# Pairing heads a and a+4: two tokens to a packet, w_in in halves of its rows, batches in half as many transfers

## The chip, the cores and the metric

The kernel runs on one core of a Trainium2 chip. A core has five engines with instruction queues of their own: TensorE (PE, matmuls), VectorE (DVE), ScalarE (ACT), GpSimd (POOL) and SyncE (SP), which here only sends transfers to the 16 DMA engines. The metric is the device time of one execution in microseconds; lower is better.

## The reference

Attention in chunks of 64 tokens, then an FFN with a SoLU and a layer norm, all in float32 (w_in and w_out are handed over as float64):

```
q, k, v: (8 batches, 8 heads, 576 tokens, 64)     chunk = 64 tokens
scores = q_c @ k_c^T / 8;  attn = softmax(scores);  out = attn @ v_c
x = out, heads side by side: (4608 tokens, 512)
h = x @ w_in                      # 512 x 1024
solu = h * softmax(h)
ln = (solu - mean) / sqrt(var + 1e-6) * g_ln
y = ln @ w_out                    # 1024 x 512
```

## The kernel before

The 4,608 tokens are 36 tiles of 128 tokens, two chunks each; nine chunks are a batch, so tile 4 (and every ninth after it) straddles two batches. All eight heads of a tile are worked on together.

Each tile goes through these steps. q and k are brought into a layout with the head dimension on the partitions (`QT`, `KT`: 128 partitions are two heads of 64, four such pairs side by side). `scores` makes 32 matmuls of 64x64x64, a softmax follows, the attention is turned, and `values` makes 32 more matmuls with v. The result is x of the tile, 512 values on four groups of 128 partitions; a group is one pair of heads, and w_in's rows are cut into four units of 128 rows to match. `ffn_in` multiplies x by w_in in 24 matmuls of 512 columns: both operands are split into a high and a low part, and three products are summed (tiles 0 and 1 take one product in plain float32 instead). SoLU, norm and turning of z follow on the other engines, and `ffn_out` makes 24 matmuls with w_out, in three thirds.

q and k reach `QT` and `KT` in one of two ways. Tiles 0 to 9 are loaded in their natural layout (`load_natural`, into the two slots of `nat`): a partition is a token, and each token and head is one run of 256 bytes. TensorE turns them (`turn_natural`, four transposes of 128x128 for q and four for k), and ScalarE or VectorE copies the result out of PSUM. From tile 10 on, whole batches are staged (`qk_loads` into `q_st` and `k_st`, two buffers each): 32 transfers a batch, one for each tensor, head and half of the head dimension, each to 32 partitions and in runs of 128 bytes; VectorE turns 32x32 blocks of them (`qk_turn`).

w_in and w_out are 4 MB each as float64. `load_pair(x)` loads a unit of 1 MB into a raw tile (x = 0 to 3 is w_in, 4 to 7 w_out; unit 0 in two transfers of half the columns). `unit_scale`, `unit_round`, `unit_high` and `unit_rest` turn a unit into its float32 value and its parts, on GpSimd, VectorE and ScalarE.

What runs when is written out by hand. Every engine works through its instructions in program order. Up to the fifth tile the order is the string `START`: each word is a step and its arguments, looked up in `todo`, and a word that comes again resumes that step behind its next `yield`. `n:i` loads natural tile i, `N:i:x` turns its q or k, `P:x` loads a unit, `v:i` loads v, `S` scores, `A`, `B` softmax, `T` turns the attention, `V` values, `M` FFN-in (M:0 in four parts, one for each unit, so it needs all four units by its end), `X`, `Y`, `z` SoLU and z, `F` a third of FFN-out, `Q:b` lists a batch's transfers and `q:n` sends n of them, `W` are matmuls with no use but to keep TensorE busy. All loads but a few go through SyncE, in the order of these words. `early` holds the two transfers of unit 0, which the words `P0` and `P1` send.

From tile 5 on a loop does the rest. An iteration sends v of a later tile, `LOADS[0]` transfers of the batch list, then FFN-in, scores and values for two tiles in every second iteration, `LOADS[1]` more transfers near its end, and then the turning of z through the DMA engines (`z_t`) in every second one. In the other iterations the turned attention (`attn_t`, four transfers on SyncE, four on GpSimd) goes ahead of them. `turn` sends what is left of a batch before it is used.

The lists `NV_DVE`, `CL_DVE`, `TV_DVE` and `SUB_POOL` say which of the copies, unit steps and subtractions run on which engine.

## Time and profile before

| what | value |
|---|---|
| three runs, median (lowest to highest) | 486.51 us (484.56 to 487.1) |
| the profiled execution | 487.32 us, of which 485.5 us are the span of the instructions |
| TensorE busy | 467.4 us, 96% of the span |
| VectorE, ScalarE, GpSimd busy | 75%, 52%, 32% |
| mean granted TensorE clock | 0.989 |
| transfers | 72.57 MB in 195,076 packets, 179,208 of them under 512 bytes |

The profile is of one execution. Its page gives busy time for each engine, the span in 40 slices, the DMA queues, the chain of work that ended last and the costliest groups; other views of the same trace list who waited for whom, the instructions in order of time, and the busy time in chosen stretches. All steps are recorded through one helper, so nearly every row has the same line, L50, and rows are told apart by engine and tile. "po<-ident,nat" is a matmul into tile po from ident and nat; "SPq" rows are SyncE sending a transfer, and their length is how long SyncE was held. In the first 55 us and between 110 and 150 us TensorE has most of its idle time.

### The profile page before, as it was taken

The page shows a single profiled execution, that of the slowest core. Times are in us where ns is not written, and L with a number is a line of the kernel's source. Part 1 is how long each engine was busy: PE and PEld are TensorE (multiplying, and loading weights), DVE is VectorE, ACT ScalarE, POOL GpSimd, SP SyncE. Part 2 cuts the span into 40 slices and gives each one's busy share as a digit, 9 for nine tenths or more (in the row PEclk, how much of TensorE's full clock was granted, in tenths as well). Part 3 has the DMA queues.
Part 4 walks back from the last instruction along what each step waited for, and adds up shares of the span by engine and source line. Part 5 has one row for each costly group of instructions (what it writes and reads, how often), then busy time and mean ns, then how long its engine had stood idle before and what let it go on. Part 6 is the DMA issues. An engine that isn't in the chain of part 4 may idle for free.

```text
span 485.5 us, 11042 instructions
## 1 busy us (share of the span) xinstructions
PE 467.4 (96%) x4189; PEld 382.0 (79%) x4189; DVE 364.5 (75%) x508; ACT 252.3 (52%) x406; POOL 157.7 (32%) x304
## 2 busy tenths in 40 slices
PE   6599999999979999999999999999999999999997
PEld 5556788887868888888888888888888888888876
DVE  1879895796829797979797979797979797954431
ACT  2668883655426464646464646464545454545451
POOL 1245467250503232323232323232323232323300
PEclk9899999999988999999999999999999999999999
DMA  9998976796976878587528496867753535344211
GB/s 270 278 230 219 238 119 157 148 191 142 195 159 130 185 151 187 116 186 147 147 75 197 107 202 124 184 127 180 151 140 80 138 83 136 83 114 110 65 45 43
DMA packets 195076, 72.57 MB, mean 149 GB/s; under 512 B 179208, under 2 KB 179728, under 8 KB 194640
## 3 DMA queue, kind: packets, MB, share of 16 engines
q1 hardware_dynamic: 188608, 59.15, 56.1%
q0 software_dynamic: 6272, 12.60, 10.1%
q8 instruction: 33, 0.54, 0.5%
q14 instruction: 19, 0.16, 0.1%
q10 hardware_dynamic: 144, 0.13, 0.1%
HBM read 37.23 MB, written 9.44 MB: 96 GB/s over the span
## 4 chain that ended last, share of the span: by engine, by line
PE 77%; SPq 10%; DMA 8%; issue 2%; DVE 2%; ACT 2%; DVEq 0%; ACTq 0%
PE po L50 37%; PE ph L50 33%; SPq L50 10%; PE sx L50 4%; PE sy L50 3%; DMA nat<-in_q_dram 3%; DMA nat<-in_k_dram 2%; DMA k_st<-in_k_dram 2%; DMA attn_t<-a_b 1%; ACT z L50 1%; DVE h_nmax L50 0%; ACT z_h L50 0%; DVE z L50 0%; DVE z_l L50 0%; ACT sq L50 0%
## 5 line engine op out<-in xcount | busy, mean ns | idle before, releaser
L50 PE MATMUL po<-wo_l,z_h 128*128 128x512 f32 x280 | 112.1, 400 | 0.1
L50 PE MATMUL po<-wo_h,z_l 128*128 128x512 f32 x280 | 110.3, 394 | 0.0
L50 PE MATMUL po<-wo_h,z_h 128*128 128x512 f32 x280 | 110.0, 393 | 0.0
L50 ACT ACTIVATE z<-ph,h_nmax 128x1024 f32<-128x1024 f32 x36 | 40.2, 1117 | 133.9 <-DVE h_nmax L50 133.7
L50 PE MATMUL ph<-wi_l,x_h 128*128 128x512 f32 x272 | 106.0, 390 | 0.0
L50 PE MATMUL ph<-wi_h,x_h 128*128 128x512 f32 x272 | 105.8, 389 | 0.0
L50 POOL TENSOR_TENSOR u<-ssq,eps 128x1 f32<-128x1 f32 x36 | 6.8, 190 | 223.3 <-ACT sq L50 223.2
L50 POOL DMA_DIRECT2D z_t<-z_b x136 | 67.8, 506 | 17.4 <-DVE z_b L50 14.6
L50 PE MATMUL ph<-wi_h,x_l 128*128 128x512 f32 x272 | 72.7, 389 | 0.0
L50 DVE TENSOR_REDUCE h_nmax<-ph 128x1 f32<-128x1024 f32 x36 | 44.0, 1223 | 31.3 <-PE ph L50 31.3
L50 PEld LDWEIGHTS po<-wo_l,z_h 128*128 128x128 f32 x280 | 53.1, 190 | 12.0 <-ACT z_h L50 0.5
L50 PEld LDWEIGHTS po<-wo_h,z_l 128*128 128x128 f32 x280 | 53.0, 189 | 11.6 <-DVE z_l L50 0.4
L50 PEld LDWEIGHTS po<-wo_h,z_h 128*128 128x128 f32 x280 | 53.2, 190 | 10.6
L50 PEld LDWEIGHTS ph<-wi_h,x_l 128*128 128x128 f32 x272 | 51.0, 188 | 10.6
L50 PEld LDWEIGHTS ph<-wi_l,x_h 128*128 128x128 f32 x272 | 51.1, 188 | 10.6
L50 PEld LDWEIGHTS ph<-wi_h,x_h 128*128 128x128 f32 x272 | 51.1, 188 | 10.6
L50 DVE TENSOR_TENSOR z_l<-z_t,z_h 128x1024 fp32r<-128x1024 f32 (+1 forms) x35 | 40.6, 1161 | 20.2 <-ACT z_h L50 20.2
L50 DVE SCALAR_TENSOR_TENSOR z<-ph,z 128x1024 f32<-128x1024 f32 x36 | 43.9, 1219 | 13.3 <-ACT z L50 13.3
L50 ACT ACTIVATE z<-z,z_sum 128x1024 f32<-128x1024 f32 x34 | 39.2, 1153 | 22.2 <-DVE z L50 21.6
L50 DVE STREAM_TRANSPOSE z_b<-z 128x1024 f32<-128x1024 f32 x33 | 40.0, 1211 | 9.6 <-POOL z L50 3.4
L50 ACT ACTIVATE o_sb<-po,r 128x512 f32<-128x512 f32 (+1 forms) x36 | 24.3, 675 | 31.5 <-POOL r L50 24.4
L50 ACT ACTIVATE sq<-z 128x1024 bf16<-128x1024 f32 x36 | 37.6, 1043 | 0.4 <-POOL z L50 0.4
(85 smaller groups left out, 627.5 us busy)
## 6 DMA issues: line engine op xcount, KB each, us to landing
out_dram<-o_sb SPq DMA_DIRECT2D x35, 256.0 KB, 2.5
z_t<-z_b SPq DMA_DIRECT2D x128, 64.0 KB, 3.0
z_t<-z_b POOLq DMA_DIRECT2D x128, 64.0 KB, 2.9
v_sb<-in_v_dram SPq DMA_DIRECT2D x27, 256.0 KB, 4.0
q_st<-in_q_dram SPq DMA_DIRECT2D x96, 72.0 KB, 3.1
k_st<-in_k_dram SPq DMA_DIRECT2D x96, 72.0 KB, 3.0
w_raw<-in_moe_w_out_dram SPq DMA_DIRECT2D x4, 1024.0 KB, 7.8
attn_t<-a_b POOLq DMA_DIRECT2D x60, 64.0 KB, 3.9
```

What stands on the lines that cost most here:

```text
L50: ins = make(*args, **kwargs)
```

## The change

Heads are paired as (a, a+4) instead of (2a, 2a+1). So a group of 128 rows of x, and with it a unit of w_in, is made of two blocks of 64 rows that lie apart in w_in, and each block is its own transfer to 64 partitions; unit 0 is cut the same way and no longer by columns. Two heads that follow each other now lie side by side on the same partitions of the staged batch, so one transfer brings both: 16 a batch, of 144 KB, and `LOADS` goes from (4, 5) to (2, 3).

Natural tiles 0 to 5 are loaded with two tokens in a run of 512 bytes: q goes to partitions 0 to 63, k to 64 to 127. `turn_pairs` (word `E`) turns q and k together by 32 matmuls of 64 rows and 64 columns, even and odd tokens apart, and `take_pairs` (word `H`) copies q or k out of PSUM, putting the tokens back in order. Tiles 6 to 9 keep the old way, with two transfers for each of q and k. `load_v` follows the new pairing. `START` is a new order, with two words `W` instead of five, and the engine lists are changed.

```diff
@@ START @@
 START = """
-W:1 n:0 N:0:1 W:2 N:0:0 n:1 N:0:0 W:5 N:0:1 P:2 P0 N:1:0 P1 S:0 N:1:1 W:4 A:0 c:2 P:1 N:1:0 A:0
-n:2 N:1:1 S:1 B:0 c:2 c:0 g N:2:0 c:0 C:2 c:1 c:1 C:2 C:0 C:1 A:1 W:19 v:0 n:3 B:0 T:0 N:2:0
-N:2:1 T:0 N:2:1 A:1 C:1 C:0 B:1 V:0 B:1 P:3 N:3:0 t:2 S:2 N:3:1 V:0 M:0 A:2 N:3:0 c:3 N:3:1 T:1
-T:1 S:3 D:2:1 P:4 n:4 c:3 v:1 M:0 A:3 G C:3 A:2 n:5 M:0 G C:3 c:4 M:0 P:5 A:3 B:2 N:4:1 N:4:0
-t:3 c:4 n:6 B:2 N:4:1 v:2 N:4:0 V:1 v:3 B:3 B:3 X:0 T:2 T:2 P:6 X:0 Y:0 C:4 N:5:0 C:4 S:4 N:5:0
...
+n:0 n:1 E:0 P:1 P0 H:0:1 H:0:0 P1 S:0 E:1 A:0 A:0 n:2 H:1:0 v:0 c:0 g H:1:1 c:0 c:1 B:0 c:1 S:1
+A:1 n:3 A:1 E:2 B:0 P:2 W:1 C:0 H:2:1 H:2:0 C:1 T:0 C:1 W:2 P:3 T:0 B:1 n:4 E:3 B:1 c:2 C:0 S:2
+t:1 P:4 V:0 H:3:1 H:3:0 A:2 V:0 T:1 M:0 T:1 c:2 D:1:0 C:2 c:3 c:3 M:0 n:5 C:2 t:2 S:3 E:4 A:2
+C:3 M:0 C:3 H:4:1 G P:5 A:3 v:1 B:2 G P:6 H:4:0 M:0 A:3 t:0 v:2 E:5 B:3 S:4 t:3 X:0 D:2:1 D:2:0
+H:5:0 X:0 H:5:1 B:2 c:4 T:2 c:4 B:3 T:3 D:0:0 n:6 c:5 V:1 n:7 D:3:0 V:1 A:4 Y:0 S:5 Y:0 v:3 T:2
+M:1 A:5 C:4 N:6:0 T:3 c:5 C:4 t:4 A:4 C:5 A:5 N:7:0 N:6:0 D:4:0 C:5 B:4 N:7:0 V:2 c:6 P:7 B:4
...
@@ -83,11 +82,11 @@
     assert FF == 32 * 32
-    NV_DVE = ((1, 1), (6, 1), (9, 1),)
+    NV_DVE = ((0, 0), (0, 1), (1, 0), (3, 0), (5, 1), (6, 1), (9, 1),)
     MEAN_POOL = (3, 4,)
-    CL_DVE = (1, 3, 4, 5,)
-    TV_DVE = (2,)
-    SUB_POOL = ((0, 0), (0, 1), (1, 0), (1, 1), (2, 0), (2, 1), (3, 0), (3, 1), (7, 0), (7, 1),)
+    CL_DVE = (3,)
+    TV_DVE = (1, 4,)
+    SUB_POOL = ((0, 0), (0, 1), (1, 0), (1, 1), (2, 0), (2, 1), (3, 0), (3, 1), (6, 0), (7, 0), (7, 1),)
     NORM_POOL = (0, 1, 2, 3, 4, 5, 6, 7,)
     SH_POOL = ()
     XV_DVE = ()
@@ -150,16 +149,21 @@
         src = (w_in, w_out)[x // NCC]
         m = x % NCC
         if x < NCC:
-            dst, src = raw.rearrange("p x a b -> p (x a b)"), src[m * P:(m + 1) * P, :]
+            dst = raw.rearrange("p x a b -> p (x a b)")
+            parts = [
+                (dst[j * D:(j + 1) * D], src[(j * HP + m) * D:(j * HP + m + 1) * D, :])
+                for j in range(2)
+            ]
         else:
             dst = raw.rearrange("p x a b -> p x (a b)")
             src = src[2 * m * P:2 * (m + 1) * P, :].rearrange("(x p) n -> p x n", x=2)
+            parts = [(dst, src)]
         if x == 0:
-            for n in range(2):
-                cols = slice(n * HALF * raw_words, (n + 1) * HALF * raw_words)
-                early[n:n] = [(dst[:, cols], src[:, cols])]
-        else:
-            sync.dma_start(dst, src)
+            early.extend(parts)
+        else:
+            for to, of in parts:
+                sync.dma_start(to, of)
         raws[x] = raw
     scaled, tops = {}, {}
@@ -236,7 +240,7 @@
-    QT, KT, V, QS, KS = {}, {}, {}, {}, {}
+    QT, KT, QK, V, QS, KS = {}, {}, {}, {}, {}, {}
     AT = const.tile([P, 2, 2, H, 32], F32, name="attn_t")
     def qk_tiles(i):
@@ -247,17 +251,19 @@
         def load(t, src, h, db):
-            p0 = (h % 2) * D + db * 32
+            p0 = h // HP * D + db * 32
             sync.dma_start(
-                t[p0:p0 + 32, h // 2, :, :],
-                src[b, h, :, db * 32:db * 32 + 32].rearrange("(g t) d -> t g d", t=32),
+                t[p0:p0 + 32, h % HP:h % HP + 2, :, :].rearrange("p a g d -> p (a g) d"),
+                src[b, h:h + 2, :, db * 32:db * 32 + 32].rearrange(
+                    "h (g t) d -> t (h g) d", t=32
+                ),
             )
         loads = []
         for src, dst, name in ((q, QS, "q_st"), (k, KS, "k_st")):
             t = stage.tile([P, HP, G, 32], F32, name=name)
             dst[b] = t
             loads += [
-                (load, t, src, h, db) for h in range(H) for db in range(2)
+                (load, t, src, h, db) for h in range(0, H, 2) for db in range(2)
             ]
         return loads
@@ -292,12 +298,26 @@
     def load_natural(i):
+        if i < PAIRS:
+            to = nat[:, i % 2].rearrange("p x h d -> p (x h d)")
+            to = to.rearrange("p (h e) -> p h e", h=H)
+            for x, src in enumerate((q, k)):
+                for p0, p1, b, s in tile_parts(i):
+                    sync.dma_start(
+                        to[x * CH + p0 // 2:x * CH + p1 // 2],
+                        src[b, :, s:s + p1 - p0, :].rearrange("h (p s) d -> p h (s d)", s=2),
+                    )
+            return
         for x, src in enumerate((q, k)):
             for p0, p1, b, s in tile_parts(i):
-                sync.dma_start(
-                    nat[p0:p1, i % 2, x],
-                    src[b, :, s:s + p1 - p0, :].rearrange("h t d -> t h d"),
-                )
+                to = nat[p0:p1, i % 2, x].rearrange("p (a j) d -> p a j d", j=2)
+                for j in range(2):
+                    sync.dma_start(
+                        to[:, :, j],
+                        src[b, j * HP:(j + 1) * HP, s:s + p1 - p0, :].rearrange("h t d -> t h d"),
+                    )
     def load_v(i):
         V[i] = work.tile([P, H, D], F32, name="v_sb", bufs=4)
@@ -310,13 +330,40 @@
             for j, p0, p1, b, s in parts:
                 sync.dma_start(
                     V[i][p0:p1, j * HP:(j + 1) * HP, :],
-                    v[b, j::2, s:s + p1 - p0, :].rearrange("h t d -> t h d"),
+                    v[b, j * HP:(j + 1) * HP, s:s + p1 - p0, :].rearrange("h t d -> t h d"),
                 )
             return
         for p0, p1, b, s in tile_parts(i):
             sync.dma_start(
                 V[i][p0:p1], v[b, :, s:s + p1 - p0, :].rearrange("h t d -> t h d")
             )
+    PAIRS = 6
+    def turn_pairs(i):
+        qk_tiles(i)
+        t = nat[:, i % 2].rearrange("p x h d -> p (x h d)")
+        t = t.rearrange("p (h s d) -> p h s d", h=H, s=2)
+        QK[i] = [bank().rearrange("p (a s t) -> p a s t", s=2, t=CH) for _ in range(2)]
+        for hp in range(HP):
+            for s in range(2):
+                for j in range(2):
+                    for x in range(2):
+                        rows = slice(x * CH, (x + 1) * CH)
+                        pe.matmul(
+                            QK[i][x][j * D:(j + 1) * D, hp, s],
+                            t[rows, j * HP + hp, s],
+                            ident[rows, rows],
+                            start=True,
+                            stop=True,
+                        )
+    def take_pairs(i, x):
+        to = (QT, KT)[x][i].rearrange("p a (t s) -> p a s t", s=2)
+        if (i, x) in NV_DVE:
+            dve.tensor_copy(out=to, in_=QK[i][x])
+        else:
+            act.copy(to, QK[i][x])
     def turn_natural(i, x):
         if i not in QT:
@@ -452,7 +499,7 @@
                     rows = slice(row * CH, (row + 1) * CH)
                     pe.matmul(
                         s[j * D:(j + 1) * D, c, hp],
-                        V[i][rows, j * HP + hp if i < TURNS else h, :],
+                        V[i][rows, j * HP + hp, :],
                         AT[rows, :, i % 2, h, :],
                         start=True,
                         stop=True,
@@ -710,10 +757,10 @@
     def load_first():
         load_pair(0)
-        sync.dma_start(*early[0])
+        load_second()
     def load_second():
-        sync.dma_start(*early[1])
+        sync.dma_start(*early.pop(0))
     def load_g():
         sync.dma_start(g_row, g_ln.rearrange("(a p) -> a p", p=P))
@@ -776,7 +823,7 @@
     todo = {
         "P": load_pair, "P0": load_first, "P1": load_second, "n": load_natural,
         "v": load_v, "g": load_g, "G": turn_g, "Q": load_batch, "q": load_some,
-        "N": turn_natural, "S": scores, "A": start_softmax, "B": softmax_b,
+        "N": turn_natural, "E": turn_pairs, "H": take_pairs, "S": scores, "A": start_softmax, "B": softmax_b,
         "T": attn_transpose, "U": attn_turn, "V": start_values, "c": unit_scale,
         "C": unit_round, "t": unit_high, "D": unit_rest, "M": ffn_in, "X": solu_a, "Y": solu_b,
         "R": variance, "Z": z_turn, "z": z_half, "F": product, "o": start_store, "W": warm,
@@ -793,7 +840,7 @@
             next(step, None)
     first = 5
-    LOADS = (4, 5)
+    LOADS = (2, 3)
     next_batch = 3
     def turn(m):
```

14 lines of the change are left out of this document (6 added, 8 removed).

## Prediction

> **What bounds the kernel now.** I read the page first, then what TensorE waited for, then the chain of waits, then the timelines of TensorE, SyncE and VectorE at the places those named, and last the transfers' rates in single stretches.
>
> ```profile
> span 485.5 us, 11042 instructions
> PE 467.4 (96%) x4189; PEld 382.0 (79%) x4189; DVE 364.5 (75%) x508; ACT 252.3 (52%) x406; POOL 157.7 (32%) x304
> ```
>
> ```profile
> PE po L50 <- DMA nat<-in_q_dram: 5.4, 3, 3.4
> PE po L50 <- DMA nat<-in_k_dram: 3.0, 2, 2.6
> PE sy L50 <- DVE kT L50: 2.4, 1, 2.4
> PE sx L50 <- ACT e L50: 1.3, 1, 1.3
> PE sx L50 <- DMA attn_t<-a_b: 0.9, 2, 0.6
> ```
>
> The first two rows are the page's, the next five list what TensorE waited for over the whole run (us, times, longest). TensorE is busy for 467.4 of 485.5 us, and nearly all that it waits for are transfers: the natural q and k tiles, the staged batches (kT is made from k_st), and the turned attention. A time can change only in those waits. The chain of waits dates them. Two rows of it from the late run:
>
> ```profile
> 169.09 1.23 PE sx L50 x61
> 193.29 1.23 PE sx L50 x61
> ```
>
> Two tiles take 193.29 - 169.09 = 24.20 us there, matmul after matmul. What is left at 169 is untouched by the change and has no TensorE wait to give. TensorE's timeline shows the same scores at the head of the three pairs before:
>
> ```profile
> 89.48 0.69 PE L50 MATMUL sx<-kT,qT 64*64 64x64 f32 x32
> 113.66 0.69 PE L50 MATMUL sx<-kT,qT 64*64 64x64 f32 x32
> 139.09 0.69 PE L50 MATMUL sx<-kT,qT 64*64 64x64 f32 x32
> 143.12 1.01 PE L50 MATMUL sy<-kT,qT 64*64 64x64 f32 x26 [2.42 <-DVE kT L50]
> ```
>
> From 89.48 to 169.09 are 79.61 us where three pairs need 72.60: **7.0 us are lost at the start of the loop**, 1.2 at 114 to 115 (attn_t), the rest from 139 on (k_st), including a slow clock after it:
>
> ```profile
> 140.00:150.00 10.00, 7.58 (x107) 6.32 (x108) 7.20 (x10) 3.07 (x5) 0.00 (x0) 0.66 0.80 149
> ```
>
> ```profile
> 98.05 5.86 SPq L50 DMA_DIRECT2D q_st<-in_q_dram  x9
> 111.40 2.54 SPq L50 DMA_DIRECT2D attn_t<-a_b  x4
> 120.95 6.35 SPq L50 DMA_DIRECT2D k_st<-in_k_dram  x9
> 136.50 3.69 SPq L50 DMA_DIRECT2D k_st<-in_k_dram  x5
> ```
>
> (The first fence is one stretch: busy time of the five engines, then granted clock 0.66, DMA share, GB/s.) SyncE's timeline says why: it sends nine loads of 72 KB each iteration, 0.65 to 0.71 us apiece, and the last of batch 3 leave only at 140, right before their use. The other loss is ahead of the loop, where the transfers are behind:
>
> ```profile
> 3.75 2.54 SPq L50 DMA_DIRECT2D w_raw<-in_moe_w_in_dram  x4
> 18.38 1.48 SPq L50 DMA_DIRECT2D w_raw<-in_moe_w_in_dram  x1
> 25.87 0.69 DVE L50 TENSOR_SCALAR w_a<-w_raw 128x1024 f32<-128x1024 f32 x1 [1.19 <-DMA w_raw<-in_moe_w_in_dram]
> 28.49 3.70 PE L50 MATMUL ph<-w_a,x_f 128*128 128x512 f32 x8
> 36.89 7.11 PE L50 MATMUL ph<-w_a,x_f 128*128 128x512 f32 x16
> 54.96 0.63 PE L50 MATMUL po<-ident,nat 128*128 128x128 f32 x4 [0.99 <-DMA nat<-in_q_dram]
> ```
>
> The last quarter of w_in leaves SyncE at 18.38 and is there at 25.87, where VectorE has waited 1.19 us for it. The first tile's FFN-in (M:0) ends with it at 28.49 + 3.70 = 32.19, the second's (M:1) at 44.00. After that TensorE runs without a gap but for 0.99 us at 54.
>
> **The change part by part.** *Rates first*, from four stretches in which one kind of transfer fills the DMA engines: 4.2 to 6.2 (natural tile 1, 256-byte packets, 128 partitions), 10 to 14 (w_in, 8 KB rows, 128 partitions), 27 to 29 (natural tile 4, whose four transfers go to 64 partitions each, halves in turn) and 64 to 65 (a batch, 128-byte packets, 32 partitions):
>
> ```profile
> DMA packets 1753, 0.45 MB, mean 225 GB/s; under 512 B 1752, under 2 KB 1752, under 8 KB 1752
> DMA packets 337, 1.71 MB, mean 428 GB/s; under 512 B 32, under 2 KB 32, under 8 KB 224
> DMA packets 1026, 0.29 MB, mean 143 GB/s; under 512 B 1018, under 2 KB 1018, under 8 KB 1026
> DMA packets 1137, 0.14 MB, mean 141 GB/s; under 512 B 1137, under 2 KB 1137, under 8 KB 1137
> ```
>
> The third row decides for me. With the same packets, transfers that fill only half of the partitions ran at 143 instead of 225 GB/s, although the next transfer in the queue went to the other half: the halves did not overlap. The change makes *every* transfer of w_in, and of natural tiles 0 to 5, such a half.
>
> The Trainium skill says the same in "SBUF — State Buffer", section "Door 1: The DMA port swizzle (why `[64,N]` ≈ `[32,N]`)": the rate goes by how many of the 16 ports the partitions reach, and 64 adjacent partitions reach 8. By it, half of its 435 GB/s, the four units of w_in would take an estimated 19.3 us. "DMA: Bandwidth & Descriptors", section "Rules for kernel authors", adds that transfers to disjoint partition halves serialize. The 143 GB/s agrees with both; by the page's rate the sum below would be 1.8 us higher.
>
> *w_in.* Four units of 1.05 MB, 4.19 MB. At 428 GB/s 9.8 us. As halves: 214 GB/s at worst (half of 428), 19.6 us; by the ratio of the rows, 143/225, 272 GB/s, 15.4 us; at best 428, no loss. I take 240 GB/s, between the first two: 17.5 us, **+7.7**.
>
> *Natural tiles 0 to 5.* A tile is 0.52 MB, 2.3 us at 225 GB/s. Packets of 512 bytes to half of the partitions are not in this trace; the bounds are 143 (as 256 bytes to halves, 3.7 us) and 428 (1.2 us). I take 179, the middle of 143 and 214: 2.9 us, +0.6 a tile. Ahead of unit 3 stand tiles 0 to 3 in both orders: **+2.3**. The units stand ahead of the same things in another order (two of them behind tile 2, the first v and tile 3), but the set that must land before M:0 ends is the same, so unit 3 is there 10.0 us later, at 35.9, and M:0 ends at 42.2.
>
> *What follows M:0.* In the new order M:1 needs V:1, whose v is behind tile 4, unit 4, tile 5 and unit 5: 2.9 + 2.4 + 2.9 + 2.4 us, and 1.5 for itself (half of it at 225, half at 143 GB/s). Unit 3's data end some 1.4 us before 35.9, so v arrives at 34.4 + 12.2 + 1.0 = 47.6 (the 1.0 is landing). V:1, S:5 and M:1 follow: 0.6 + 0.6 + 7.1, M:1 ends at 55.9 instead of 44.0, +11.9. It has S:5 behind it, which came after M:1 before (0.6), and the 0.99 us wait at 54 is covered by then. **Before the loop: 11.9 - 0.6 - 1.0 = +10.3 us.**
>
> *Turning two tokens at once.* Rows of the old way and of the nearest thing to the new one:
>
> ```profile
> 32.59 1.06 PE L50 MATMUL po<-ident,nat 128*128 128x128 f32 x8 [0.40 <-DMA nat<-in_k_dram]
> 22.43 0.69 PE L50 MATMUL sx<-kT,qT 64*64 64x64 f32 x32
> 8.11 0.59 ACT L50 COPY qT<-po 128x512 f32<-128x512 f32 x1 [6.09 <-PE po L50]
> 11.78 0.68 DVE L50 COPY kT<-po 128x512 f32<-128x512 f32 x1
> ```
>
> A tile's eight turns (1.06) become 32 matmuls of the shape of scores (0.69): 0.4 us less, six times; these lie where TensorE waits for data, and the walk above holds what shows. The copies keep their sizes, now written every second word: between 0.6 us and twice that, on engines that wait for the same data; I take 0.6. The new step waits for q and k together, with scores queued behind it; the old first turn took k, the later of the two in the queue, so this wait is no longer. Moving copies between VectorE, ScalarE and GpSimd is hidden in the same way, and so are the three pairs of warming matmuls left out. If M:0 ran at a 0.66 clock after a long wait, as at 140 us, it would lose up to 2.
>
> *Natural tiles 6 to 9* go out as two transfers for each of q and k: 8 issues more, at some 0.5 us on SyncE, ahead of v and w_out loads that then wait for the DMA engines anyway. Nothing, at most +1.
>
> *The batches.* 16 transfers of 144 KB instead of 32 of 72 KB, 5 an iteration instead of 9. A batch's bytes need the same 2.36 MB / 141 GB/s = 17 us of the DMA engines, but SyncE's part halves: from 98.05 to the last load of batch 3 it sends 32 loads, then 16. That a larger load costs SyncE no more shows in the very first one, 256 KB:
>
> ```profile
> 0.72 0.45 SPq L50 DMA_DIRECT2D nat<-in_q_dram  x1
> ```
>
> So I keep 0.5 to 0.7 us an issue: 8 to 11 us of SyncE's 42 are freed, and the last load leaves at the head of its iteration, not its middle. What is late by at most 3.5 us (139.6 to 143.1) is then in time, attn_t no longer stands behind nine loads, and the clock does not drop: **-7.0**. Bounds: 0 if the DMA engines and not the issue set the end, -7.0 as nothing more is lost. A later TensorE, as forecast, widens the cover, so I take the whole.
>
> Sum: +10.3 - 7.0 = **+3.3 us**. The profiled execution took 487.3 us (485.5 of span); the runs' median is 486.5, 0.8 below it. 486.5 + 3.3 = 489.8; I say **490**.
>
> **Rivals.**
>
> *Full rate for the halves* (the other side). If two neighbouring halves do overlap, w_in costs nothing more and the tiles at 428 GB/s gain 1.1 us each, 4.4 us up to unit 3. Place: the first 26 us. -4.4 - 7.0 = -11.4: **475**. For it: 8 KB packets to halves are not in the trace, and the 143 is of 256-byte packets. Against: that row itself. Point: the loss before the loop is w_in's extra plus 2.6 (2.3 for the tiles, 1.9 as M:1 is 11.9 and not 10.0 late, less 0.6 and 1.0), so it equals 7.0 at an extra of 4.4 us, 14.2 us for w_in, 295 GB/s. Above that rate the change gains.
>
> *Half an overlap*: engines drift apart, w_in at 320 GB/s (+3.3), the tiles at 225 as before (0): 3.3 + 1.0 for v - 1.6 = +2.7; -7.0 makes -4.3: **482**.
>
> *The two sides cancel*: w_in at the ratio's 272 (+5.6), the tiles at 214 (+0.5), 1.9 - 1.6 behind: +6.4 - 7.0: **486**.
>
> *The stall in the loop stays*: a 144 KB load holds the queue for about 1 us at 141 GB/s, and attn_t and z_t stand behind two or three of them. The engines' 141 against an issue every 0.5 us speaks for it, the bytes ahead (up to 432 KB, from 360) against. +10.3 and only -3: **494**. It is also the case in which M:0 meets the slow clock.
>
> **How the numbers follow.** The forecast 0.38, alone 488 to 493; full rate 0.15; half overlap 0.17; cancelled 0.21; stall stays 0.09. This kernel's measurement can tell about 0.5%, 2.4 us, from no change. Faster: 0.15 and nearly all of 0.17, 0.31. Same: 0.21 and a rest, 0.22. Slower: 0.38 + 0.09 = 0.47. For the range: 494 plus 2 for a slow clock is the top, the bottom reaches into the full-rate case: 477 to 496.
>
> **What would show it.** Right: while w_in loads, 64-partition transfers at 210 to 280 GB/s; M:0's end past 38 us and M:1's past 50; no wait of TensorE for kT or attn_t after 90 us, pairs 24.2 us apart from the first on. Wrong: w_in near 400 GB/s, or M:1 ending at 44 or sooner (then the full-rate case), or the kT wait still there. The 512-byte packets themselves must show as 6 tiles with half the packets; if not, the first part of the change did nothing.

## The result, and the profile after

The changed kernel takes 493.17 us in the median of six runs (lowest 492.22, highest 493.72), the kernel before 486.50 beside it on the same chip: ratio 1.0148, 95% interval 1.0117 to 1.0178. It is slower by 6.7 us (7.2 by the ratio), twice the 3.3 us of the forecast's sum. A few executions ran longer as a whole and are left out of all ratios, among them the profiled one of `e17_second_all` below (775.77 us at a TensorE clock of 0.57), of which no row is shown. The profiled execution took 492.22 us, 4.9 more than that of before.

Two rows of the page after, and the list of what TensorE waited for (us, times, longest):

```profile
span 490.4 us, 11599 instructions
PE 466.3 (95%) x4513; PEld 380.7 (78%) x4513; DVE 366.6 (75%) x509; ACT 248.9 (51%) x401; POOL 163.5 (33%) x309
```

```profile
PE po L49 <- DMA nat<-in_q_dram: 12.0, 3, 5.5
PE po L49 <- DMA nat<-in_k_dram: 3.0, 3, 1.2
PE sx L49 <- issue: 2.0, 2, 1.6
PE sx L49 <- DVE qT L49: 1.4, 1, 1.4
PE sx L49 <- ACT kT L49: 1.1, 1, 1.1
```

TensorE's busy time is that of before within 1.1 us. Its waits for natural q have grown from 5.4 to 12.0 us, and the waits for kT and attn_t in the loop are gone; "issue" is a wait for nothing that the profile names. The chain of waits has the scores at the head of the loop's pairs:

```profile
101.54 1.20 PE sx L49 x61
125.73 1.20 PE sx L49 x61
174.16 1.20 PE sx L49 x61
```

The first head is 12.0 us later than before (89.48), the fourth 5.1 later (169.09), so the start lost 12.0 and the loop gained 7.0: three pairs take 72.6 us. TensorE's and VectorE's timelines show the start, and the transfers' rate from 8 to 15 us, while w_in loads, is the last row:

```profile
36.45 0.29 PE L49 MATMUL po<-ident,nat 64*64 64x64 f32 x2 [1.67 <-DMA nat<-in_q_dram]
37.96 1.81 PE L49 MATMUL po<-ident,nat 64*64 64x64 f32 x62 [1.22 <-DMA nat<-in_k_dram]
39.70 2.92 PE L49 MATMUL ph<-w_a,x_f 128*128 128x512 f32 x4
42.71 1.98 PE L49 MATMUL ph<-w_a,x_f 128*128 128x512 f32 x4
48.24 0.33 PE L49 MATMUL sy<-attn_t,v_sb 64*64 64x64 f32 x4 [0.41 <-DMA v_sb<-in_v_dram]
48.73 0.93 PE L49 MATMUL sy<-attn_t,v_sb 64*64 64x64 f32 x27 [0.16 <-DMA v_sb<-in_v_dram]
50.40 7.13 PE L49 MATMUL ph<-w_a,x_f 128*128 128x512 f32 x16 [0.21 <-ACT x_f L49]
```

```profile
35.07 0.69 DVE L49 TENSOR_SCALAR w_a<-w_raw 128x1024 f32<-128x1024 f32 x1 [1.40 <-DMA w_raw<-in_moe_w_in_dram]
```

```profile
DMA packets 240, 1.57 MB, mean 225 GB/s; under 512 B 48, under 2 KB 48, under 8 KB 48
```

w_in runs at 225 GB/s instead of 428, its last unit is there at 35.07 instead of 25.87, and the second tile's FFN-in (M:1) ends at 57.5 instead of 44.0. Between them TensorE waits for tile 4 (first two rows), and only then comes the rest of M:0.

### The profile page after: what moved, and what is told of

The parts are those of the page before. It is cut to its first block, busy times and chain, and to the rows that moved or that the text cites. A ratio compares the mean times of both kernels' runs of the same rounds, so it can differ in the third digit from the quotient of the medians.

```text
span 490.4 us, 11599 instructions
## 1 busy us (share of the span) xinstructions
PE 466.3 (95%) x4513; PEld 380.7 (78%) x4513; DVE 366.6 (75%) x509; ACT 248.9 (51%) x401; POOL 163.5 (33%) x309
## 2 busy tenths in 40 slices
DMA packets 187446, 72.60 MB, mean 148 GB/s; under 512 B 165560, under 2 KB 172224, under 8 KB 186880
## 4 chain that ended last, share of the span: by engine, by line
PE 88%; DMA 8%; DVE 1%; SPq 1%; issue 1%; ACT 0%; DVEq 0%; ACTq 0%
PE po L49 41%; PE ph L49 39%; DMA v_sb<-in_v_dram 5%; PE sx L49 5%; PE sy L49 3%; DMA w_raw<-in_moe_w_in_dram 3%; SPq L49 1%; DMA nat<-in_k_dram 1%; DVE h_nmax L49 1%; ACT z L49 0%; DVE kT L49 0%; DVE s_sum L49 0%; ACT z_h L49 0%; ACT x_f L49 0%; DVE o_sb L49 0%
## 5 line engine op out<-in xcount | busy, mean ns | idle before, releaser
L49 POOL DMA_DIRECT2D z_t<-z_b x136 | 67.7, 505 | 18.5 <-DVE z_b L49 16.8
L49 PEld LDWEIGHTS ph<-wi_l,x_h 128*128 128x128 f32 x272 | 51.1, 188 | 10.8 <-DVE z L49 0.2
L49 PEld LDWEIGHTS ph<-wi_h,x_l 128*128 128x128 f32 x272 | 51.1, 188 | 10.6
L49 PEld LDWEIGHTS ph<-wi_h,x_h 128*128 128x128 f32 x272 | 51.1, 188 | 10.5
L49 ACT ACTIVATE o_sb<-po,r 128x512 f32<-128x512 f32 (+1 forms) x36 | 24.2, 673 | 31.0 <-POOL r L49 22.1
```

The lines of the kernel that those rows point to most:

```text
L49: ins = make(*args, **kwargs)
```

## The experiments

Each time below is a median, with its ratio to the kernel before on the same chip and the interval of the ratio.

**The halves of w_in, and what makes them slow.** First they were added alone to the kernel before (`e1_halves`); then each half was put on every second partition (`e16_second`).

```diff
+            parts = [(dst[j * D:(j + 1) * D], src[j * D:(j + 1) * D, :]) for j in range(2)]
...
-            sync.dma_start(dst, src)
+            for to, of in parts:
+                sync.dma_start(to, of)
```
```diff
-            parts = [(dst[j * D:(j + 1) * D], src[j * D:(j + 1) * D, :]) for j in range(2)]
+            parts = [(dst[j:P:2], src[j * D:(j + 1) * D, :]) for j in range(2)]
```

> The kernel before with one part of the change alone: each unit of w_in in two transfers of 64 partitions, one after the other from SyncE; pairing, natural tiles, batches and order stay as before. Theory A (transfers to half of the partitions run at about half the rate, and neighbouring halves do not overlap): 8 KB packets take about 600 ns instead of 313, w_in loads at 210 to 240 GB/s, the last unit reaches VectorE 7 to 9 us after 25.87, the second tile's FFN-in ends at 50 to 53 us instead of 44.0. Part of that is given back, since a later TensorE covers the 7 us stall in the loop: 488 to 494 us in all. Rival B (the halves cost nothing, the loss of the changed kernel lies in its new order and its turning by small matmuls): 486 to 487 us, w_in near 420 GB/s, FFN-in of the second tile at 44.

> The kernel with the half transfers of w_in alone (493.2), but each half is written to every second partition, the first to the even ones and the second to the odd ones: still 64 partitions a transfer, now over the whole height of the buffer. The rows of w_in then meet other rows of x, so the output is not the reference's; every instruction, byte and packet size is the same. Theory A, 64 adjacent partitions reach half of the ports and that halves the rate: w_in runs near 400 GB/s, the second tile's FFN-in ends near 44 instead of 53, and the time is 486 to 488. Theory B, a transfer of 64 rows as such is slow (too few packets in flight on the queue): still near 220 GB/s and 492 to 494.

Halves alone: 493.20, 1.0153 (1.0121 to 1.0186). On every second partition: 487.73, 0.9987 (0.9952 to 1.0023). M:1 in the timeline and the rate from 10 to 14 us, first of the halves alone, then of the spread ones:

```profile
45.86 7.10 PE L50 MATMUL ph<-w_a,x_f 128*128 128x512 f32 x16
```

```profile
DMA packets 133, 0.85 MB, mean 213 GB/s; under 512 B 29, under 2 KB 29, under 8 KB 29
```

```profile
39.78 7.11 PE L50 MATMUL ph<-w_a,x_f 128*128 128x512 f32 x16
```

```profile
DMA packets 254, 1.69 MB, mean 422 GB/s; under 512 B 48, under 2 KB 48, under 8 KB 48
```

Number, bytes, packet sizes and order of the transfers are the same in both. So 64 rows as such do not slow w_in; 64 *adjacent* partitions halve the rate. The queue's packets fill the 16 DMA engines' time in both stretches (101.7% and 101.5% of it), so each packet takes twice as long, and the share of busy engines does not tell. M:1 ends at 46.9 in the spread run, not near the 44 that I had expected; why was not settled, and the time differs from that of before by no more than its interval. The Trainium skill, "SBUF — State Buffer", section "Door 1: The DMA port swizzle (why `[64,N]` ≈ `[32,N]`)", says that the rate goes by the ports that the partitions reach; by its table 64 adjacent ones reach 8 and every second one all 16. 213 against 422 GB/s agrees.

**Two queues.** The second half of each unit leaves from ScalarE's queue (`e3_two_queues`), and k of tiles 0 to 5 as well (`e7_both_queues`).

```diff
-            for to, of in parts:
-                sync.dma_start(to, of)
+            for n, (to, of) in enumerate(parts):
+                (act if n else sync).dma_start(to, of)
...
-                    sync.dma_start(
+                    (sync, act)[x].dma_start(
```

> The changed kernel, but the second half of each unit of w_in is sent from ScalarE's queue instead of SyncE's, so that the two halves are in flight side by side. Theory A (two DMA engines share a port while one half is written, the other ports idle): both halves together near 400 GB/s, 8 KB packets back to some 320 ns, the first two units there 4 to 5 us sooner, the last one 8 to 9; the second tile's FFN-in ends near 50 instead of 57.4, and the loop gains as much: 484 to 487 us. Rival B (packets or descriptors of such a transfer are slow in themselves, or the engines are at their limit): the rate stays at 220 GB/s and the time at 492 to 494.

> The changed kernel with the second half of each unit of w_in and k of natural tiles 0 to 5 sent from ScalarE's queue, so that q and k of a tile, too, are written side by side. Theory A: beside what the w_in halves give, a tile takes 1.3 to 1.6 us instead of 2.5; the first tile is turned 1 us sooner, tiles 2 to 5 some 2 to 5 us; 481 to 485 us, below both kernels. Rival B: as the changed kernel, 492 to 494. Rival D (waits of ScalarE for a free slot hold its copies): between the two, 485 to 490, with ScalarE idle ahead of its transfers.

Both gain nothing on the changed kernel (1.0148): 497.81, 1.0246 (1.0177 to 1.0314), slower but with an interval that meets the other's, and 498.80, 1.0274 (1.0239 to 1.0309), clearly slower. ScalarE's timeline and TensorE's waits in the first:

```profile
0.73 1.21 ACTq L49 DMA_DIRECT2D w_raw<-in_moe_w_in_dram  x2
```

```profile
PE sx L49 <- issue: 10.2, 2, 6.0
```

ScalarE's halves of the first two units left ahead of tile 0, and its queue moved nothing between 9 and 20 us, while SyncE's halves of these units loaded; so this run could not tell what it was made for. It shows what such a queue may cost: TensorE waited 10.2 us for nothing that is named. In the second run k of tiles 0 and 1 goes ahead on ScalarE's queue, and from 9 to 13 us both queues carry halves of w_in side by side:

```profile
DMA packets 169, 1.12 MB, mean 281 GB/s; under 512 B 32, under 2 KB 32, under 8 KB 32
```

281 GB/s is more than the 225 of halves one after the other, and far from the 400 of my Theory A: two queues give back only a part. The run lost elsewhere: TensorE waits for natural q and k for 19.1 us, 15.0 in the changed kernel.

**The natural tiles.** `e10_rows` is the changed kernel with a unit of w_in as 128 rows in one transfer again; `e12_rows_nat` also loads tiles 0 to 5 with one token a packet to 128 partitions, the turning left as it is.

```diff
-            parts = [
-                (dst[j * D:(j + 1) * D], src[(j * HP + m) * D:(j * HP + m + 1) * D, :])
-                for j in range(2)
-            ]
+            parts = [(dst, src[m * P:(m + 1) * P, :])]
...
-                        to[x * CH + p0 // 2:x * CH + p1 // 2],
-                        src[b, :, s:s + p1 - p0, :].rearrange("h (p s) d -> p h (s d)", s=2),
+                        nat[p0:p1, i % 2, x],
+                        src[b, :, s:s + p1 - p0, :].rearrange("h t d -> t h d"),
```

> The changed kernel with each unit of w_in as 128 rows in a row again, one transfer to all 128 partitions (unit 0 in two of half the columns). The rows then belong to other heads than x's, so what it computes is not the reference's; the amount of work and every other step are those of the changed kernel. Theory A (halves of w_in are the whole loss): w_in at 410 to 428 GB/s, second tile's FFN-in ends at 46 to 49 us instead of 57.4, pairs 24.2 us apart, 481.5 to 485 us, below the kernel before. Rival B (the new order, the 64 records of small matmuls a tile and the colder clock cost as well): 486 to 490 us.

> The changed kernel and its order, with each unit of w_in as 128 rows in a row (not the reference's output), and natural tiles 0 to 5 loaded as before, one token and head a packet of 256 bytes on all 128 partitions, while the turning stays that of two tokens (so q and k are garbled as well). Against the same kernel with two-token packets (490.9): Theory H1 (their half-partition transfers delay the turns, that of tile 4 above all): 484 to 488 us, tile 4 turned by 32 us instead of 36.7. Theory H2 (the turning's instructions and the cold clock cost, not the packets): 489.5 to 492.

Neither output is the reference's. 490.92, 1.0086 (1.0045 to 1.0126), and 485.25, 0.9982 (0.9957 to 1.0006). With w_in fast the changed kernel gains only 2.3 us, and since the runs spread from 487 to 494 us the intervals overlap; with the natural tiles changed too it gains another 5.7, clear of both. TensorE's timeline around tile 4, first of w_in in rows:

```profile
32.91 0.98 PE L49 MATMUL po<-ident,nat 64*64 64x64 f32 x32 [1.74 <-DMA nat<-in_k_dram]
35.61 1.13 PE L49 MATMUL po<-ident,nat 64*64 64x64 f32 x30 [1.72 <-issue]
36.67 3.61 PE L49 MATMUL ph<-w_a,x_f 128*128 128x512 f32 x4
```

then with one-token packets:

```profile
30.44 1.14 PE L49 MATMUL po<-ident,nat 64*64 64x64 f32 x58 [0.43 <-DMA nat<-in_k_dram]
31.51 1.98 PE L49 MATMUL ph<-w_a,x_f 128*128 128x512 f32 x4
```

Tile 4's k comes 2.5 us later with two-token packets (32.91 against 30.44), TensorE then waits 1.7 for nothing named in the middle of the turn, the turn itself is 1.0 longer (0.98 + 1.13 against 1.14), and the slowed clock makes M:0's third quarter 1.6 longer (3.61 against 1.98): 6.8 us at its end, of which 5.3 are left at the first head (98.07 against 92.81).

That changed the packets' size and the partitions at once. `e17_second_all` is the changed kernel in which every transfer to 64 adjacent partitions goes to every second one, and nothing else; `e19_pairs_reach` has w_in, pairing and turned tiles 6 to 9 of before, the new order, and two-token packets spread in the same way, turned from all 128 rows.

```diff
-                        to[x * CH + p0 // 2:x * CH + p1 // 2],
+                        to[x + p0:p1:2],
```
```diff
-                            t[rows, j * HP + hp, s],
-                            ident[rows, rows],
+                            t[:, 2 * hp + j, s],
+                            ident[:, x:P:2],
```

> The changed kernel, in which every transfer that goes to 64 adjacent partitions goes to every second partition instead: the halves of w_in to the even and the odd ones, q of natural tiles 0 to 5 to the even and k to the odd ones. Number, order, bytes and packet sizes of all transfers are the same, and so is every instruction of every engine; the rows meet other rows, so the output is not the reference's. Theory A, the loss is the reach of the partitions alone: w_in near 400 GB/s, the two-token packets above 300 GB/s, tile 4 turned by 31.5 us, FFN-in of the second tile ends before 49 and the time is 482 to 486 (one-token packets on 128 partitions with w_in in rows gave 485.25). Theory B, packets of 512 bytes or transfers of 64 rows cost something whatever they reach: 488 to 492, the natural tiles near 220 GB/s. Theory C, the 64x64 turning and the instructions it adds hold TensorE up: the data are there and TensorE still waits at the second tile's scores for nothing that the profile names, 486 to 489.

> The kernel with the new order alone (484.68, ratio 0.9941: old transfers, 16 batch transfers) and one thing more of the change: q and k of natural tiles 0 to 5 in two tokens a packet, q on the even and k on the odd partitions, turned in 32 matmuls a tile; heads stay paired 2a, 2a+1, w_in in rows of 128 partitions. The output is the reference's. Theory A, the two-token packets cost only by the 64 partitions they reach in the changed kernel: at full reach within 1 us of 484.7 or below it, 482 to 485.7, packets of 512 bytes at 260 to 300 GB/s. Theory B, the 64 small matmuls and their instructions, or the 512-byte packets themselves, cost: 487 to 490, with TensorE waiting at the second tile's scores for nothing that the profile names.

The first: 488.24, 0.9996 (0.9952 to 1.004). Against the changed kernel's 1.0148 the destination partitions alone are worth 1.5%, **7.4 us, as much as the whole loss**. That fits a loss by reach, though 488.24, the median of all executions, lay where I had put a cost of the packets, and the rates that I had forecast for this run are not shown. The second: 486.41, 0.9991 (0.9964 to 1.0018), between my two ranges. Its rate from 3 to 6 us and its TensorE:

```profile
DMA packets 1678, 0.83 MB, mean 278 GB/s; under 512 B 52, under 2 KB 1678, under 8 KB 1678
```

```profile
32.15 3.59 PE L49 MATMUL po<-ident,nat 128*64 128x64 f32 x64 [3.16 <-DMA nat<-in_k_dram]
45.32 7.10 PE L49 MATMUL ph<-w_a,x_f 128*128 128x512 f32 x16 [0.54 <-DVE z L49]
```

512-byte packets at full reach run at 278 GB/s, in the changed kernel at 231. They bring nothing here: the run is 0.5% behind the same order with the old tiles (0.9941, below), with intervals that just meet. A turn over 128 rows takes 3.59 us there instead of 1.81, both at a slowed clock (2.16 against 1.16 for tile 5 at full clock), which would account for it; that is argued, not shown.

A version with the reference's output and w_in at full reach was tried too (`e18_reach`): one transfer a unit, whose source is two blocks of 64 rows.

```diff
+            both = src.rearrange("(j a d) n -> a j d n", j=2, a=HP)[m]
+            parts = [(dst, both)]
```

> The changed kernel made to reach all partitions with the reference's output: a unit of w_in is one transfer whose source is two blocks of 64 rows (the first unit two transfers, each of half the columns), q of natural tiles 0 to 5 lies on the even partitions and k on the odd ones, two tokens a packet as in the changed kernel, and a turn takes all 128 rows against every second column of the identity, 32 matmuls as in the changed kernel. Theory A, reach alone: 481 to 486, below the changed kernel by 7 us or more, FFN-in of the second tile ends before 49. Theory B, the packets or the turning cost something by themselves: 487 to 491. If q and k in packets of 512 bytes run faster than the 225 GB/s of the 256-byte ones and the start gains by it, 478 to 482.

556.26, 1.1426 (1.1371 to 1.1482), a clear miss. SyncE's timeline, and the rate from 10 to 14 us:

```profile
3.61 19.09 SPq L49 DMA_DIRECT2D w_raw<-in_moe_w_in_dram  x3
```

```profile
DMA packets 27, 0.23 MB, mean 57 GB/s; under 512 B 0, under 2 KB 0, under 8 KB 0
```

```profile
q1 hardware_dynamic: 26, 0.21, 12.7%
```

57 GB/s is about an eighth of the 428 of one transfer of 128 rows, and the queue's packets took 12.7% of the 16 DMA engines' time in this stretch, as much as two of them have. The Trainium skill, "DMA: Bandwidth & Descriptors", section "Why a DMA increments its semaphore by 16 and not by 1", says that the number of engines follows the slowest dimension of the access pattern; here that was 2.

**The batches in 16 transfers.** Alone on the kernel before (`e9_before16`; from tile 10 on heads are paired a, a+4 up to the values, which put them back), and the changed kernel with 32 of 72 KB again (`e4_32loads`).

```diff
-                (load, t, src, h, db) for h in range(H) for db in range(2)
+                (load, t, src, h, db) for h in range(0, H, 2) for db in range(2)
...
-    LOADS = (4, 5)
+    LOADS = (2, 3)
```

> The kernel before with the batches' part of the change alone: for the staged tiles (10 to 35) heads are paired as (a, a+4), a batch goes out in 16 transfers of 144 KB, five an iteration; values puts each head back to where w_in as it was wants it, so w_in, the natural tiles and the order of the first steps stay. Theory A (SyncE's issuing set the stall of 7 us at the loop's start): the waits for attn_t and kT at 115 and 143 us are gone, pairs 24.2 us apart from the first on, 479.5 to 482.5 us. Rival E (the DMA engines' 141 GB/s for these packets set it, and half as many transfers carry the same bytes): waits of the same size at the same place, 485 to 487.5 us.

> The changed kernel with batches in 32 transfers of 72 KB again, nine an iteration, as before. Theory A (the 7 us stall of the loop was SyncE's issuing, and the 16 transfers took it away): TensorE waits again for kT or attn_t near 130 to 155 us, heads of pairs 1 to 4 us further apart than 24.2, 495 to 500 us. Rival C (the late start of the changed kernel alone covers the stall, as SyncE has 12 us more): heads of pairs 24.2 us apart, 492.5 to 494 us.

Alone: 484.13, 0.9953 (0.9925 to 0.9982), **0.5% faster than the kernel before**, and so faster than both. Undone in the changed kernel: 492.81, 1.0143 (1.0114 to 1.0173), no change. SyncE's timeline and the chain of the latter:

```profile
78.91 10.15 SPq L49 DMA_DIRECT2D k_st<-in_k_dram  x16
```

```profile
101.83 1.20 PE sx L49 x61
174.44 1.20 PE sx L49 x61
```

32 transfers, and no stall: 72.6 us for three pairs. I put this down to the later start, which gives the loads more time. `e11_rows32` did the same in the run with w_in in rows:

> As the run before it in this list (w_in's units in 128 rows in a row, so the output is not the reference's), and batches in 32 transfers, nine an iteration. With the early start given back, Theory A (SyncE's issuing) has the stall return: 3 to 7 us above that run. Rival C (what removed the stall in the changed kernel was its order or its late start, not the number of transfers): within 1 us of it.

492.17, 1.0109 (1.0068 to 1.0149), heads at 96.05 and 24.2 apart: no stall with an earlier head either. Then the changed kernel in the old order of first steps, with the halves (`e13_oldstart`) and with w_in in rows (`e14_oldstart_rows`).

```diff
-n:0 n:1 E:0 P:1 P0 H:0:1 H:0:0 P1 S:0 E:1 A:0 A:0 n:2 H:1:0 v:0 c:0 g H:1:1 c:0 c:1 B:0 c:1 S:1
...
+W:1 n:0 E:0 W:2 n:1 H:0:0 W:5 H:0:1 P:2 P0 E:1 P1 S:0 W:4 A:0 c:2 P:1 H:1:0 A:0 n:2 H:1:1 S:1 B:0 c:2
...
-    CL_DVE = (3,)
+    CL_DVE = (1, 3, 4, 5,)
...
```

> The changed kernel with the order of the first steps and the engine lists of the kernel before: where that order turned a tile's q or k by transposes, the new step turns both, and the copies stand where they stood; halves of w_in, two-token packets and 16 transfers stay. Theory A (halves of w_in set the end of the first steps, whatever the order): 491.5 to 495 us, FFN-in of the second tile at 52 to 58. Theory G (the new order itself is a second cause of the size of the halves: it puts the turn of tile 4 ahead of the last half of the first FFN-in, and leaves TensorE cold): 487 to 490.5, FFN-in of the second tile by 51.

> As the run before it in this list, with the order of the kernel before, and each unit of w_in as 128 rows in a row in one transfer (so rows meet other heads of x, and what it computes is not the reference's). What is left of the change is two-token packets with their turning, and the 16 transfers. Theory A (halves alone cost): 481 to 485 us, as the kernel before with 16 transfers (484.1) or better. Theory H (two-token packets and the 32 small matmuls a tile cost by themselves, by half-partition transfers, and by more instructions to be fetched): 486 to 491 us, with TensorE waiting for natural tiles or for nothing that the profile names.

498.28, 1.0243 (1.0182 to 1.0304), and 490.65, 1.0085 (1.0045 to 1.0124). SyncE's and TensorE's timelines of the first:

```profile
107.08 4.86 SPq L48 DMA_DIRECT2D k_st<-in_k_dram  x4
```

```profile
105.20 0.69 PE L48 MATMUL sx<-kT,qT 64*64 64x64 f32 x32
181.70 0.69 PE L48 MATMUL sx<-kT,qT 64*64 64x64 f32 x32
```

A head 16 us later than before, and 3.9 us of stall (76.50 - 72.60): a late start does not cover it. (In the old order, by the ratios, the halves of w_in cost 1.6%, 1.0243 against 1.0085, and the two-token packets with their turning 1.3%, 1.0085 against the 0.9953 of 16 transfers alone.) All runs together tell what does. "Sent" is when SyncE has sent the last load of the first staged batch, from the head of the first pair (for the changed kernel in the old order 107.08 + 4.86 - 105.20); "lost" is what three pairs take over 72.6 us:

| kernel | order, transfers | first head | sent | lost |
|---|---|---|---|---|
| before | old, 32 | 89.48 | 7.9 after | 7.0 |
| halves of w_in alone | old, 32 | 97.97 | 8.3 after | 6.1 |
| 16 transfers alone | old, 16 | 89.70 | 7.1 after | 3.8 |
| changed, old order | old, 16 | 105.20 | 6.7 after | 3.9 |
| changed, old order, w_in in rows | old, 16 | 97.42 | 5.9 after | 2.9 |
| changed | new, 16 | 101.47 | 14.4 ahead | 0 |
| changed, 32 transfers | new, 32 | 101.76 | 12.7 ahead | 0 |
| w_in in rows, 32 transfers | new, 32 | 96.05 | 12.5 ahead | 0 |

In the new order the words `q:4` that send the first batch stand earlier. So they were moved alone: forward in the old order (`e20_sooner`, with 16 transfers) and back in the changed kernel (`e21_later`).

```diff
-v:6 B:6 Z:3 o:0 z:1:1 z:1:0 z:1:1 B:6 R:3 X:4 F V:5 q:4 N:9:0 N:9:0 X:4 F N:9:1 U:6 U:7 R:1 F
-Y:4 q:4 o:1 N:9:1 Y:4 o:1 R:4 q:4
...
+c:6 T:5 S:6 q:4 V:3 D:5:0 V:4 q:4 X:2 C:6 N:7:0 N:7:1 T:5 q:4 c:7 X:2 F N:7:1 C:6 V:4 q:4 Y:2 N:8:0 c:7 t:6
```

> The kernel before with the batches in 16 transfers (484.13 alone) and one thing more: the four words q:4, which send the first batch, stand earlier in the order, at the places relative to the scores and FFN steps that they have in the changed kernel; everything else keeps the old order. The output is the reference's. Theory A, the loop's loss comes from the first batch leaving after the loop has begun (old order: its last load is out 7.1 us after the scores at the head of the loop's first pair, and 3.8 us are lost with 16 transfers; new order: 14 us before, and nothing is lost, with 16 or with 32 transfers): its last load is out before that head, pairs stand 24.2 us apart from the first on, and the time is 480 to 483 if the sooner loads delay nothing else. Theory B, the later start of TensorE is what covers the loads: the loss of 3 to 4 us stays, 484 to 485. Theory C, the loads now collide with the natural tiles, v and w_out: the head comes later by as much as the loop gains, 483.5 to 486.

> The changed kernel with its four words q:4, which send the first batch, moved back to the end of the order of first steps, where they stand in the kernel before; nothing else differs. Theory A, the place of these words removes the loop's loss: it is back, 3 to 4 us over the first three pairs, the time 494 to 498. Theory B, the later start of TensorE or the 16 transfers remove it: pairs stay 24.2 us apart and the time stays at 492 to 494.

Back: 501.24, 1.031 (1.0271 to 1.0349), 8.1 us more than the changed kernel. TensorE's timeline, and a row of its waits:

```profile
102.83 0.69 PE L47 MATMUL sx<-kT,qT 64*64 64x64 f32 x32
135.00 0.69 PE L47 MATMUL sx<-kT,qT 64*64 64x64 f32 x32
```

```profile
PE sx L47 <- DMA attn_t<-a_b: 5.8, 2, 5.5
```

The first pair takes 32.2 instead of 24.2 us, twice the stall I had expected. Forward: 487.93, 1.0031 (1.0001 to 1.0061). SyncE's and TensorE's timelines, and the stretch from 80 to 90 us (five engines, clock, DMA share, GB/s):

```profile
67.94 8.53 SPq L48 DMA_DIRECT2D k_st<-in_k_dram  x8
```

```profile
83.75 1.09 PE L48 MATMUL po<-ident,nat 128*128 128x128 f32 x4 [4.48 <-DMA nat<-in_q_dram]
95.90 0.69 PE L48 MATMUL sx<-kT,qT 64*64 64x64 f32 x32
168.50 0.69 PE L48 MATMUL sx<-kT,qT 64*64 64x64 f32 x32
```

```profile
80.00:90.00 10.00, 6.25 (x23) 5.14 (x24) 3.63 (x6) 2.91 (x6) 4.10 (x8) 0.66 0.82 167
```

The stall is gone (168.50 - 95.90 = 72.60), but natural tile 9, queued behind the batch on SyncE, is now late: TensorE waits 4.48 us for it, the clock falls to 0.66, and the first head comes 6.2 us later than with 16 transfers alone. So the words' place removes the stall, and at these places in the old order they cost more at the start than the loop gains.

**What the new order is worth.** The kernel with 16 transfers alone, in the new order and with the new engine lists (`e15_neworder`).

> The kernel before with the batches in 16 transfers (that alone measured 484.13) and the changed kernel's order of first steps and choice of engines; the natural tiles and w_in keep the transfers of before (256-byte packets and 8 KB rows, all 128 partitions), and a tile is turned as before, eight turns of 128x128. The output is the reference's. Theory A, the new order is worth something by itself (with the half transfers it was worth 5.1 us: 498.28 in the old order, 493.17 in the new): the second tile's FFN-in ends before 44.0, 480 to 483.5. Theory B, it only lets the late transfers be borne better and is worth nothing where none is late: 484 to 486, FFN-in of the second tile ends at 44 to 49. Theory C, with data on time the turning as 64x64 matmuls is what cost the run with w_in in rows and one-token packets (485.25) its remaining microseconds: then this one is below that run by 1 us or more, and TensorE's unnamed waits at the second tile's scores, 1.6 to 1.7 us in the changed kernel, are gone.

484.68, 0.9941 (0.9916 to 0.9966). Its timeline of TensorE:

```profile
44.01 7.11 PE L48 MATMUL ph<-w_a,x_f 128*128 128x512 f32 x16 [0.52 <-DVE z L48]
95.06 0.69 PE L48 MATMUL sx<-kT,qT 64*64 64x64 f32 x32
167.72 0.69 PE L48 MATMUL sx<-kT,qT 64*64 64x64 f32 x32
```

With every transfer as before, the new order brings M:1's end to 51.1 and the first head to 95.06, 5.6 us later than before, and loses nothing in the loop. Beside 16 transfers alone (0.9953) that is no difference: it moves the loss from the loop to the start. My third expectation, a gain of 1 us or more on the run with one-token packets, is not shown: the intervals overlap (0.9941 and 0.9982), and that run, which turns by the small matmuls, has the sooner first head (92.81) and no wait for nothing named either.

**The clock.** The changed kernel has fewer matmuls that only keep TensorE busy; 18 pairs were put back (`e5b_warm`, words `W` ahead of `E:0` and behind `S:1`).

```diff
-n:0 n:1 E:0 P:1 P0 H:0:1 H:0:0 P1 S:0 E:1 A:0 A:0 n:2 H:1:0 v:0 c:0 g H:1:1 c:0 c:1 B:0 c:1 S:1
+n:0 n:1 W:1 W:2 W:3 W:4 W:5 W:6 E:0 P:1 P0 H:0:1 H:0:0 P1 S:0 E:1 A:0 A:0 n:2 H:1:0 v:0 c:0 g H:1:1 c:0 c:1 B:0 c:1 S:1 W:1 W:2 W:3 W:4 W:5 W:6 W:7 W:8 W:9 W:10 W:11 W:12
```

> The changed kernel with 18 more pairs of warming matmuls: 6 ahead of the first turn, 12 behind the scores of tile 1, where TensorE waits for tile 2. Theory A (the first 45 us are set by transfers, a cold clock lies beside them): small turns and scores take 1.2 and 0.7 us instead of 2.0 and 1.1, but the second tile's FFN-in still ends at 56.5 to 57.5; 492 to 493.5 us. Theory F (the cold clock is what the sum lacked): FFN-in of the second tile ends 2 us sooner or more, 489 to 491.5 us.

497.25, 1.0238 (1.019 to 1.0287): slower than the changed kernel by 4 us, and outside both ranges. TensorE waits 9.2 us in all for nothing named, 2.0 in the changed kernel, and M:1 ends at 61.1; so the run says nothing for or against the clock. (With four more pairs behind the scores of tile 3, `e5_warm`, the program deadlocks and has no time.)

## Why the prediction was right or wrong

The sign and the range were right, the size was half. **The term that was too small is "+10.3 before the loop": the first head shows +12.0.** With the 7.0 that the loop gained, as forecast, this makes the 5.1 us that the profiled executions show at the fourth head, where 3.3 were forecast. The rest of the 6.7, some 1.7 us, is where these two executions stand to their medians, 0.8 above it before and 0.95 below it after; no trace shows where it lies, and it stays open.

The signs that were named for "right" came: w_in below 280 GB/s, M:0's end past 38 and M:1's past 50, no wait for kT or attn_t in the loop, pairs 24.2 us apart. The last two had another cause than the one given.

- *w_in at 240 GB/s, +7.7.* The term was mis-sized: 213 to 225 GB/s. At 224 the 4.19 MB take 18.7 us, +8.9. The mechanism, adjacent halves at half rate, is shown by the halves on every second partition; the bound that I set at half of 428 was the right value. It excludes the 272 and 320 GB/s of the rivals "the two sides cancel" and "half an overlap".
- *Natural tiles at 179 GB/s, +2.3 up to unit 3.* Mis-sized the other way: alone (3 to 6 us) the packets run at 231, as fast as the 256-byte ones before, and 25.87 + 8.9 = 34.8 already gives unit 3 at 35.07. The two errors cancelled to 0.8 us, which is luck. What the packets cost lies elsewhere: tile 4.

```profile
DMA packets 1394, 0.69 MB, mean 231 GB/s; under 512 B 43, under 2 KB 1394, under 8 KB 1394
```

- *M:0 ends with unit 3, at 42.2.* This step failed, though it did not set the end of M:1. "The set that must land before M:0 ends is the same" overlooked TensorE's own order: in the new one E:4 stands ahead of M:0's third quarter. The last of tile 4 was waited for until 37.96, E:4 took 1.81, the quarter at a slowed clock 2.92, and M:0 ended at 44.7. TensorE still waited 0.41 us for v behind it, so an M:0 at 42.2 would only have lengthened that wait.
- *v at 47.6, M:1 ends at 55.9, +10.3 before the loop.* This is the step that made the sum too small. v was waited for until 48.24, 0.6 later, and its second part until 48.73; V:1 and S:5 then took until 50.40, 2.16 us where the sum had 1.2. So M:1 ended at 57.5, 1.6 late, and the head shows +12.0. The path was right, 1.7 short. But it booked 10.0 of its 11.9 on rates. With the old transfers the new order alone is 5.6 us late at the first head; the other 6.4 come with the transfers. That a sum split so differently came this near is in part luck.
- *Turning, 0.4 less a tile.* Wrong by a misreading, which the description of the kernel before shares: scores, and values too, are 16 matmuls, each two records, so the 32 turns are 64 records. A tile takes 1.16 us, or 1.98 at a slow clock, not 0.69: 0.1 more than the 1.06 of the eight transposes, not 0.4 less.
- *Batches, -7.0.* Right in size, wrong in its cause. It said that SyncE's issues halve, since a larger load costs SyncE no more. SyncE's rows of the changed kernel:

```profile
78.83 8.23 SPq L49 DMA_DIRECT2D k_st<-in_k_dram  x8
124.94 6.54 SPq L49 DMA_DIRECT2D k_st<-in_k_dram  x5
142.54 0.58 SPq L49 DMA_DIRECT2D k_st<-in_k_dram  x1
144.41 1.74 SPq L49 DMA_DIRECT2D q_st<-in_q_dram  x3
```

  In a row of eight or five one costs 1.0 to 1.3 us, against 0.71 for one of half the size before (6.35 for nine); the single one, and each of the three from 144.41 on, costs 0.58. That the dear ones wait for loads ahead of them in the queue fits this, but is argued. The sixteen loads of the next batch hold SyncE for 18.5 us in all, the thirty-two before held it for 21.7: not half. Sixteen transfers alone take away 3.2 of the 7.0. What takes all of it is that the first batch is sent ahead of the loop, which moving those words alone shows; the "wider cover" of a late start does not, as the old order with a head at 105.20 shows. I had not seen the words' new place as part of the change.
- *The rivals.* "Full rate, 475" was priced wrong. Full reach was measured: the ratio is 0.9996. The rate was not the only thing that made the start longer; the order's 5.6 us belong in that sum, and no run shows the 4.4 us that the tiles were to gain. An estimate from the runs, -7.0 + 5.6, is 485.1 us, within the interval of that ratio. "The stall stays" did not come.
- *The extra issues of tiles 6 to 9 and the moved copies* were not tried by themselves.

## What to carry to other kernels

Split a transfer by columns or by every second partition rather than into 64 adjacent ones: here these halved the rate, and what was queued behind them came late too. (No run here has w_in at full reach together with the new pairing and the reference's output at a good time; the one that tried, with a source of two blocks, took 63 us more than the changed kernel.) When an order of first steps changes, walk each engine's own order, and look up where every queue's words now stand, before pricing rates. A stall that vanishes may have been moved: compare the heads of the steady loop, not the wait.

## What the runs showed of the hardware that I had not expected

- 64 partitions at 422 GB/s, when they are every second one.
- One transfer with a source of two blocks at 57 GB/s, and SyncE held for 19.09 us by three of them.
- Two queues that carry the two halves of w_in side by side at 281 GB/s, between 225 and 428.
- TensorE's waits for nothing named, 2.0 us in all in the changed kernel (the longest 1.6) and 10.2 with w_in on two queues. With the new order there are none where tiles 0 to 5 went to all 128 partitions, by old packets (with either turning) or by spread ones; but `e7_both_queues`, with 64 adjacent partitions, has none either. Their cause was not settled.
- SyncE is held 0.58 to 1.3 us by a load of the same 144 KB in the changed kernel.
